# Two PSUM tiles of one bank each for the attention values and the softmax denominators, in place of one tile of two banks

## The chip, the cores and the metric

The kernel runs on one core of a Trainium2 chip. The metric is the time of one execution in microseconds (us) on the device, lower is better. A profile is one further execution, recorded by the hardware profiler. The engines are PE (TensorE, matmuls), PEld (its weight loads), DVE (VectorE), ACT (ScalarE), POOL (GpSimd) and SP (SyncE, which issues all DMAs here).

## What is computed

Attention over a band of neighbours and block summaries, then a GELU feed-forward layer on the result (the inputs q and k are scaled up by 8):

```python
k_sum = k.reshape(B, H, nb, 32, D).max(axis=3); v_sum = v.reshape(B, H, nb, 32, D).mean(axis=3)
scores_l = where(|i - j| < 16, q @ k.T / sqrt(D), -1e9)
scores_s = q @ k_sum.T / sqrt(D) + log(32)
a = softmax(concatenate([scores_l, scores_s], axis=-1))
x = a @ concatenate([v, v_sum], axis=2)          # B, H, S, D = 4, 8, 768, 64
h = x.reshape(B * S, 512) @ w_in                 # 512 x 2048
return gelu(h) @ w_out                           # 2048 x 512
```

## The kernel before

**Tiling.** The 3072 rows are cut into 12 chunks of 256 rows. Attention is done in 24 units: one unit is 4 heads of one chunk, so two units make a chunk's 512 columns of x. All products are made of 16-bit parts: an operand a is held as hi(a) + lo(a), and a product is three matmuls (hi hi, hi lo, lo hi).

**Steps of one unit**, by the names of the ORDER string. `scores u` (L653, 48 matmuls) fills the two-bank PSUM tile ps_s. ACT (`evac`, L659) or DVE (`add_mask`, L662) copies it out to s32, POOL takes the maximum over the partitions (`maximum`, L670, one buffer m32), DVE subtracts it (`shift`, L675), ACT takes the exponential (`exponent`, L678) and rounds it to 16 bits (`s_p_hi`, L684), DVE makes the rest (`p_lo`, L687). Then PE makes two things of p:

- `values u` (L717, 48 matmuls) writes the weighted sum of v into the columns 0 to 511 of the PSUM tile ps_v: its first bank.
- `den u` (L725, 4 matmuls with a matrix of ones) writes the denominators, spread over 64 partitions each, into the columns 512 to 1023 of ps_v: its second bank. 14 of the 24 units do this (0 to 7, 9 to 13 and 16). The other ten sum the denominators on POOL (`pden`, L731) and copy them with L736.

The denominators leave through ACT: `norm_den u` (L741) adds eps and copies the second bank to x32, an SBUF tile. DVE transposes it (`norm_take`, L744), takes reciprocals (`norm_rec`, L747), spreads them back (`norm_spread`, L751), and multiplies the first bank of ps_v by them (`norm_mult`, L757), which gives x. x is split by `x_hi` (ACT, L760; L782 where the feed-forward works on sums) and `x_lo` (DVE, L766; L788).

**The feed-forward.** `phase1 c i` (L806 to L808, 24 matmuls of 256 columns) or `product` (L833, seven products in place of eight for a pair of chunks) fills one of four single PSUM banks. ACT takes the GELU (`gelu`, L854) or a copy (`keep`, L839), DVE adds (`h_add`, L845), `g_hi` (ACT, L864) and `g_lo` (DVE, L868) split it, `phase2` (L881 to L883) multiplies by w_out, and `store` (ACT, L886) and `put` (SP) write the chunk out. Weights arrive early, as 64-bit numbers, and DVE turns them into 32-bit ones with integer operations (L372, L377, L381) before they are split.

**What sets the order.** The ORDER string fixes it by hand: each engine gets its instructions in the order in which the string names the steps, and each engine executes its own in order. What an instruction waits for is set by a recording layer from the tiles that it reads and writes. PSUM has eight banks: two for ps_s, two for ps_v, and four for the ring named bank.

Some stretches of the string matter for the change. `den 6 ... scores 7 ... phase1 2 6, values 6, ... norm_den 6, g_hi 2 1, evac 7, ... scores 8` is one, where the denominators are made well ahead of the values. Unit 9 has the same shape: `den 9, ... phase1 3 3, values 9, ... norm_den 9, ... gelu 3 3, exponent 10, ... s_p_hi 10`, and later `p_lo 10, norm_mult 9, ... den 10`. Unit 3: `den 3, ... norm_den 3, ... values 3`. Unit 5: `den 5, norm_mult 4, x_hi 4, ... x_lo 4, add_mask 6, ... values 5, ... norm_den 5`.

## Time and profile before

| | us |
|---|---|
| median of 3 runs | 598.34 (596.81 to 598.61) |
| the profiled execution | 595.35 |
| its span, first to last instruction | 593.6 |
| PE busy | 578.2 (97% of the span) |
| DVE busy | 439.7 (74%) |
| ACT busy | 362.6 (61%) |
| POOL busy | 169.7 (29%) |
| mean granted TensorE clock | 0.996 |

The span is what the profile shows; the profiled execution's own time is 1.75 us more. [...] In the lists of waits, "A <- B: t, n, m" says that A's engine sat idle before A until B had ended, t us in n times, the longest m us. In the timeline a row is start, duration, engine, line, operation, and in brackets the idle time before it and what ended it. In the chain of waits a row is start, duration and the work that the end was waiting for.

### The profile page before, as it was taken

Reading aid. Unit: us, or ns where it says so; the run is one execution under the profiler, and the core shown is the slowest. Engines: PE = TensorE matmul, PEld = TensorE weight load, DVE = VectorE, ACT = ScalarE, POOL = GpSimd, SP = SyncE. Lnnn points to the kernel's source line nnn. Section 1 sums busy time; section 2 is a strip of 40 time slices with the busy share of each in tenths; the row PEclk is TensorE's granted clock in tenths of the full one; section 3 lists DMA queues with packets and bytes.
Section 4 is the critical chain, followed back from the end, with each engine's and each line's share of the span. In section 5 each row is a group of like instructions: output and inputs, shape, how many; then the busy total and the mean of one; then the engine's idle time right before and its main releaser. Section 6 shows DMA issues by size and latency. Waiting matters only on the chain.

```text
span 593.6 us, 13319 instructions
## 1 busy us (share of the span) xinstructions
PE 578.2 (97%) x5801; PEld 376.5 (63%) x5801; DVE 439.7 (74%) x544; ACT 362.6 (61%) x534; POOL 169.7 (29%) x80
## 2 busy tenths in 40 slices
PE   8999999999899999999999799999999999999997
PEld 3447787444776774588664478755678654686645
DVE  5998999997799989889868778868758665542220
ACT  3899766263776578368882578983675752345410
POOL 3231002023034423115064436453642552100000
PEclk9999999999999999999999999999999999999999
DMA  8765655556557613320231342202112100000001
GB/s 331 277 245 178 212 175 196 180 166 231 164 157 208 205 38 92 114 68 14 65 102 42 106 129 84 81 6 88 43 49 62 37 8 35 19 19 1 1 18 54
DMA packets 27306, 63.78 MB, mean 107 GB/s; under 512 B 2480, under 2 KB 6704, under 8 KB 26672
## 3 DMA queue, kind: packets, MB, share of 16 engines
q1 hardware_dynamic: 27248, 62.93, 33.2%
q8 instruction: 45, 0.74, 0.5%
q14 instruction: 13, 0.11, 0.1%
HBM read 54.86 MB, written 6.29 MB: 103 GB/s over the span
## 4 chain that ended last, share of the span: by engine, by line
PE 79%; ACT 7%; DVE 5%; DMA 3%; POOL 2%; issue 2%; SPq 1%; ACTq 0%; POOLq 0%; DVEq 0%
PE bank L833 22%; PE bank L881 11%; PE bank L883 10%; PE bank L882 10%; PE bank L806 5%; PE bank L807 5%; PE bank L808 5%; PE ps_v L717 3%; PE ps_s L653 3%; DMA v<-in_vw_dram 1%; PE ps_v L725 1%; POOL m L670 1%; DVE v_lo L693 1%; DMA w_out_l<-in_kp_first_dram 1%; POOL m L731 1%
## 5 line engine op out<-in xcount | busy, mean ns | idle before, releaser
L881 PE MATMUL bank<-w_out_h,gh 128*128 128x512 f16 x368 | 139.6, 379 | 0.0
L883 PE MATMUL bank<-w_out_h,gl 128*128 128x512 f16 x368 | 139.5, 379 | 0.0
L882 PE MATMUL bank<-w_out_l,gh 128*128 128x512 f16 x368 | 139.5, 379 | 0.0
L670 POOL PARTITION_ALL_REDUCE m<-s x24 | 82.0, 3417 | 188.4 <-ACT s L659 92.1
L868 DVE SCALAR_TENSOR_TENSOR gl<-g,gh 128x512 f16<-128x512 f32 x96 | 67.1, 712 | 40.3 <-ACT gh L864 40.3
L731 POOL PARTITION_ALL_REDUCE m<-s x10 | 62.0, 6199 | 64.6 <-ACT s L678 64.6
L833 PEld LDWEIGHTS <-w 128*128 128x128 f16 x640 | 62.0, 98 | 11.1 <-issue 1.3
L883 PEld LDWEIGHTS <-gl 128*128 128x128 f16 x368 | 36.0, 98 | 43.8 <-DVE gl L868 0.4
L833 PEld LDWEIGHTS <-w_in 128*128 128x128 f16 x576 | 55.6, 98 | 10.4 <-issue 1.8
L881 PEld LDWEIGHTS <-gh 128*128 128x128 f16 x368 | 36.0, 98 | 39.8 <-issue 1.2
L845 DVE TENSOR_TENSOR g<-bank,late 128x512 f32<-128x512 f32 x48 | 32.8, 686 | 37.5 <-PE bank L833 20.0
L882 PEld LDWEIGHTS <-gh 128*128 128x128 f16 x368 | 36.0, 98 | 38.3
L864 ACT ACTIVATE gh<-g 128x512 f16<-128x512 f32 x96 | 58.4, 624 | 1.0
L839 ACT ACTIVATE late<-bank 128x512 f32<-128x512 f32 x48 | 28.2, 590 | 45.6 <-PE bank L833 34.3
L807 PE MATMUL bank<-x,w_in 128*128 128x256 f16 x192 | 53.0, 276 | 0.8 <-DVE x L766 0.8
L806 PE MATMUL bank<-x,w_in 128*128 128x256 f16 x192 | 53.1, 276 | 0.6 <-ACT w_in L435 0.4
L808 PE MATMUL bank<-x,w_in 128*128 128x256 f16 x192 | 52.9, 276 | 0.0
L833 PE MATMUL bank<-x,w_in 128*128 128x256 f16 x384 | 46.6, 273 | 1.7 <-DVE x L788 1.6
L854 ACT ACTIVATE g<-bank 128x512 f32<-128x512 f32 x48 | 28.1, 592 | 27.8 <-PE bank L808 20.5
L833 PE MATMUL bank<-stage,w 128*128 128x256 f16 x320 | 44.0, 273 | 0.0
L833 PE MATMUL bank<-x,w 128*128 128x256 f16 x320 | 43.9, 273 | 0.0
L854 ACT ACTIVATE g<-g 128x512 f32<-128x512 f32 x48 | 29.7, 624 | 18.4 <-DVE g L845 18.1
(145 smaller groups left out, 1135.9 us busy)
## 6 DMA issues: line engine op xcount, KB each, us to landing
v<-in_vw_dram SPq DMA_DIRECT2D x24, 512.0 KB, 3.6
stage<-in_w_out_dram SPq DMA_DIRECT2D x8, 1024.0 KB
q<-in_qd_dram SPq DMA_DIRECT2D x24, 256.0 KB, 2.8
out_dram<-ot SPq DMA_DIRECT2D x23, 256.0 KB, 2.1
k<-in_kd_dram SPq DMA_DIRECT2D x18, 320.0 KB, 4.9
stage<-in_kp_dram SPq DMA_DIRECT2D x6, 768.0 KB, 4.7
stage<-in_vb_dram SPq DMA_DIRECT2D x6, 768.0 KB
stage<-in_w_in_dram SPq DMA_DIRECT2D x4, 1024.0 KB
```

The source lines that it names most:

```text
L670: nc.gpsimd.partition_all_reduce(out_ap=m32, in_ap=self.s32, channels=P, reduce_op=bass_isa.ReduceOp.max)
L731: nc.gpsimd.partition_all_reduce(out_ap=m32, in_ap=self.s32, channels=P, reduce_op=bass_isa.ReduceOp.add)
L806: nc.tensor.matmul(dst, wh, xh, start=(k == 0), stop=False)
L807: nc.tensor.matmul(dst, wh, xl, start=False, stop=False)
L808: nc.tensor.matmul(dst, wl, xh, start=False, stop=(k == NCC - 1))
L833: nc.tensor.matmul(dst, l, r[:, k], start=(first and e == 0 and k == 0 and n == 0), stop=(k == KH - 1 and n == 2), skip_group_check=True,)
L854: nc.scalar.activation(g, h, AF.Gelu, scale=1.0 / (SC_X * SC_WI))
L864: nc.scalar.activation(gh, g_ring.use(f"{c}_{i}", g_uses(c, i)), AF.Copy, scale=SC_G)
L868: nc.vector.scalar_tensor_tensor(out=gl, in0=g_ring.use(f"{c}_{i}", g_uses(c, i)), scalar=SC_G, in1=gh, op0=ALU.mult, op1=ALU.subtract)
L881: nc.tensor.matmul(t, gh[:, f, js], w_out_h[:, f, :], start=(n == 0), stop=False)
L882: nc.tensor.matmul(t, gh[:, f, js], w_out_l[:, f, :], start=False, stop=False)
L883: nc.tensor.matmul(t, gl[:, f, js], w_out_h[:, f, :], start=False, stop=(n == NFC - 1))
```

## The change

The PSUM tile ps_v of 1024 columns becomes two tiles of 512 columns, ps_v for the values and ps_d for the denominators. Each is one bank; the eight banks are used as before.

```diff
     ps_s = ps.tile([P, UCOLS], F32, name="ps_s")
-    ps_v = ps.tile([P, UCOLS], F32, name="ps_v")
+    ps_v, ps_d = (ps.tile([P, QCOLS], F32, name=n) for n in ("ps_v", "ps_d"))
...
                 for e in range(2):
                     nc.tensor.matmul(
-                        ps_v[e * D : (e + 1) * D, QCOLS:], ones, p[:, e * QCOLS : (e + 1) * QCOLS],
+                        ps_d[e * D : (e + 1) * D], ones, p[:, e * QCOLS : (e + 1) * QCOLS],
                         start=(n == 0), stop=(n == 1),
                     )
...
         def norm_den(self):
-            nc.scalar.activation(self.x32, ps_v[:, QCOLS:], AF.Identity, bias=eps)
+            nc.scalar.activation(self.x32, ps_d, AF.Identity, bias=eps)
...
-            nc.vector.tensor_tensor(out=self.x32, in0=ps_v[:, :QCOLS], in1=dent, op=ALU.mult)
+            nc.vector.tensor_tensor(out=self.x32, in0=ps_v, in1=dent, op=ALU.mult)
```

No instruction is added or removed, and the order on every engine stays. What 40 instructions wait for differs between the two programs. In the rows below a wait names the engine whose count is waited for, not the instruction; which instruction it is, is said in words. Numbers behind a name are buffer numbers and differ by one because there is a tile more.

On ACT, from the GELU ahead of `norm_den 6` (L741) to the one behind `evac 7` (L659), before:

```order
L854 ACTIVATE g_3_100<-bank_65 128x512 [waits PE_49]
L854 ACTIVATE g_0_97<-bank_66 128x512
L741 ACTIVATE den_81<-ps_v,eps 128x512 [waits PE_49]
L864 ACTIVATE gh_101<-g_0_97 128x512 [waits Activation_49]
L659 ACTIVATE s_1_91<-ps_s,logb 128x1024
L854 ACTIVATE g_2_99<-bank_64 128x512
```

and after:

```order
L854 ACTIVATE g_3_101<-bank_66 128x512 [waits PE_49]
L854 ACTIVATE g_0_98<-bank_67 128x512
L741 ACTIVATE den_82<-ps_d,eps 128x512 [waits PE_49]
L864 ACTIVATE gh_102<-g_0_98 128x512 [waits Activation_49]
L659 ACTIVATE s_1_92<-ps_s,logb 128x1024 [waits PE_49]
L854 ACTIVATE g_2_100<-bank_65 128x512 [waits PE_49]
```

Before, `norm_den 6` waits for the last matmul of `values 6`; after, for the last matmul of `den 6`. The two rows behind it had no wait of their own, since the later count covered them; now each waits for its own matmuls (`scores 7` and `phase1 2 6`). The same replacement is made for `norm_den` 5, 9, 10 and 13.

On PE, `den 10` (L725) behind a `phase2` step, before:

```order
L882 MATMUL bank_65<-w_out_l,gh_103 128x512
L883 LDWEIGHTS gl_104
L883 MATMUL bank_65<-w_out_h,gl_104 128x512
L725 LDWEIGHTS ones [waits DVE_49]
L725 MATMUL ps_v<-p_h,ones 64x512 [waits Activation_49]
L725 LDWEIGHTS ones
L725 MATMUL ps_v<-p_h,ones 64x512
L725 LDWEIGHTS ones
L725 MATMUL ps_v<-p_l,ones 64x512
```

and after:

```order
L882 MATMUL bank_66<-w_out_l,gh_104 128x512
L883 LDWEIGHTS gl_105
L883 MATMUL bank_66<-w_out_h,gl_105 128x512
L725 LDWEIGHTS ones
L725 MATMUL ps_d<-p_h,ones 64x512 [waits Activation_49]
L725 LDWEIGHTS ones
L725 MATMUL ps_d<-p_h,ones 64x512
L725 LDWEIGHTS ones
L725 MATMUL ps_d<-p_l,ones 64x512 [waits DVE_49]
```

The wait at the first weight load was for `norm_mult 9` (L757), which reads the values of the unit before. It is gone; what is left of DVE is the wait for `p_lo 10`, at the matmul that reads it. The wait for `norm_mult` of the unit before stands at the first matmul of `values 10` now. `den` 3, 9 and 11 change in the same way. `values 3` waited for `norm_den 3` and now waits for `norm_mult 2`; `values 1` likewise.

On DVE, `norm_mult 4` (L757) to `add_mask 6` (L662), before:

```order
L751 STREAM_TRANSPOSE dent<-rec 128x512 [waits DVE_49]
L757 TENSOR_TENSOR den_81<-ps_v,dent 128x512 [waits DVE_49,PE_49]
L449 TENSOR_TENSOR w_2_77<-w_2_77 128x512
L766 TENSOR_TENSOR x<-den_81,x 128x512 [waits Activation_49]
L662 SCALAR_TENSOR_TENSOR s_0_90<-mask_sb,ps_s 128x1024
```

and after:

```order
L751 STREAM_TRANSPOSE dent<-rec 128x512 [waits DVE_49]
L757 TENSOR_TENSOR den_82<-ps_v,dent 128x512 [waits DVE_49,PE_49]
L449 TENSOR_TENSOR w_2_78<-w_2_78 128x512
L766 TENSOR_TENSOR x<-den_82,x 128x512 [waits Activation_49]
L662 SCALAR_TENSOR_TENSOR s_0_91<-mask_sb,ps_s 128x1024 [waits PE_49]
```

Before, `norm_mult 4` waits for the last matmul of `den 5`, the next unit's; after, for that of `values 4`. `add_mask 6` gets a wait for `scores 6` of its own. `norm_mult` 0 and 7 change likewise.

## The prediction

> **What bounds the kernel now.** I read the page first, then PE's list of waits.

> ```profile
> span 593.6 us, 13319 instructions
> PE 578.2 (97%) x5801; PEld 376.5 (63%) x5801; DVE 439.7 (74%) x544; ACT 362.6 (61%) x534; POOL 169.7 (29%) x80
> ```

> PE is busy for all but 15.4 us of the span, and the other engines are idle for a quarter of it and more. The change takes no work off PE, so it can gain only what PE stands idle and what the idling brings with it. PE's list of waits says where that is:

> ```profile
> PE ps_s L653 <- ACT s L659: 2.3, 1, 2.3
> PE bank L833 <- DVE x L788: 1.6, 1, 1.6
> PE ps_s L653 <- DVE ql L642: 1.3, 1, 1.3
> PE ps_v L725 <- DVE stage L757: 1.3, 1, 1.3
> PE ps_v L717 <- ACT den L741: 1.2, 2, 0.8
> ...
> PE bank L807 <- DVE x L766: 0.8, 1, 0.8
> ```

> Two rows name ps_v itself: `den` waiting for `norm_mult` (1.3) and `values` waiting for `norm_den` (0.8, and the remaining 0.4). These pairs touch different halves of ps_v. The first row, the largest wait of all, and the last, for x, stand at the end of chains that start at L741. What ACT waits for ahead of L741 (the list for that line) shows it:

> ```profile
>   PE ps_v L717: 8.4, 5
>   PE ps_v L725: 0.8, 1
> ```

> L741 reads the denominators, which L725 makes, and yet it stands 8.4 us for L717, the values. So the old tile is waited for as a whole. The question is which of these 8.4 us PE pays for.

> **The change, part by part.** No work is added, so every term is a wait. I go through the places in order of time.

> *At 40 us (`values 1`).* The 0.4 us wait goes, but I count nothing for it. ACT sets this stretch: four microseconds later PE's weight load stands behind ACT's copy of v_lo.

> ```profile
> 45.03 0.41 PEld L430 LDWEIGHTS bank<-w,mask_sb 128*128 128x128 f32 x2 [0.33 <-ACT v_lo L708]
> ```

> A PE that is 0.4 us early waits 0.4 us longer there. Cover gone, this would be a gain of 0.4.

> *At 63 us (`values 3`).* The timelines of PE and ACT:

> ```profile
> 63.79 0.22 PE L717 MATMUL ps_v<-p_h,v_hi 128*64 128x64 f16 x2 [0.79 <-ACT den L741]
> ```
> ```profile
> 61.60 0.63 ACT L760 ACTIVATE x<-den 128x512 f16<-128x512 f32 x1
> ```

> Now `values 3` waits for `norm_mult 2`, whose result ACT's `x_hi 2` (L760) already read at 61.60, so nothing holds it: 0.8 us gained. PE must then find its inputs 0.8 us earlier. DVE, busy with weight bits in the stretch that follows, is the one that could refuse; the meeting that I check is `p_lo 4` (L687) for `den 4`, on DVE's timeline and in the chain:

> ```profile
> 123.19 1.22 DVE L687 TENSOR_TENSOR p_l<-s,p_h 128x1024 f16<-128x1024 f32 x1
> ```
> ```profile
> 125.61 0.55 PE ps_v L725 x4
> ```

> It ends at 124.41, while `den 4` starts on PE at 125.61. 1.2 us of slack against 0.8: the gain passes.

> *At 147 us (`x` of unit 5).* DVE's timeline, then ACT's:

> ```profile
> 136.64 0.70 DVE L751 STREAM_TRANSPOSE dent<-rec 128x512 f32<-128x512 f32 x1
> 139.01 0.69 DVE L757 TENSOR_TENSOR den<-ps_v,dent 128x512 f32<-128x512 f32 x1 [1.68 <-PE ps_v L725]
> ```
> ```profile
> 142.59 0.69 ACT L741 ACTIVATE den<-ps_v,eps 128x512 f32<-128x512 f32 x1 [1.11 <-PE ps_v L717]
> ```

> `norm_mult 4` (139.01) waited 1.68 us for `den 5`, which it doesn't read, and `norm_den 5` (142.59) for `values 5`. Both waits go: DVE is 1.68 us early up to `add_mask 6`, and ACT, free from 141.48 (it sat idle for 1.11 us ahead of 142.59), is at least 1.1 us early with the denominators. x then comes 1.1 to 2.8 us (1.68 + 1.11) early. PE stood 0.8 for it (L807), and with the 0.8 from 63 us it asks for it 1.6 us early: 0.8 gained.

> *At 160 us (`scores 8`).* The chain:

> ```profile
> 154.91 0.55 PE ps_v L725 x4
> ...
> 159.91 0.69 ACT den L741
> 160.60 0.52 ACT gh L864
> 161.12 1.01 ACT s L659
> ```
> ```profile
> 155.14 1.07 ACT L854 ACTIVATE g<-bank 128x512 f32<-128x512 f32 x2
> 159.91 0.69 ACT L741 ACTIVATE den<-ps_v,eps 128x512 f32<-128x512 f32 x1 [3.70 <-PE ps_v L717]
> ```

> `norm_den 6` holds ACT for 3.70 us although `den 6` was done at 155.46. Queued behind it on ACT are `g_hi 2 1` and `evac 7`, and `evac 7` is what frees ps_s for `scores 8`. With the new wait ACT goes on at 156.21, and 0.69 + 0.52 + 1.01 later, at 158.4, ps_s is free. PE gets to `scores 8` when `values 6` ends, just ahead of 159.91. So all 2.3 us go, with 1.5 us to spare. If PE comes 1.6 us early and ACT not at all, 0.1 of it is lost; I take 0.3 off the sum for meetings of this kind.

> The same wait has a second price, which the windows show:

> ```profile
> 159.27:162.68 3.41, 1.11 (x73) 1.08 (x69) 1.53 (x3) 2.77 (x5) 0.47 (x1) 1.00 0.41 76
> 162.68:166.09 3.41, 3.41 (x39) 2.45 (x32) 3.31 (x5) 0.97 (x2) 3.41 (x3) 0.50 0.93 254
> ...
> 333.34:336.76 3.42, 1.79 (x15) 1.29 (x14) 3.42 (x5) 0.30 (x2) 0.03 (x1) 1.00 0.00 0
> ```

> The column behind the busy times of the five engines is the granted clock. It is 0.50 for 3.41 us right behind the idle time. 3.41 us at half speed do 1.7 us of work, so 1.7 us are lost. A stretch of equal length at 333 us in which PE idled for half the time (1.79 busy) was followed by no drop; the one at 159 us with two thirds idle was. With the wait gone the drop should go: 1.7 gained.

> [...]

> *At 227 us (`den 10`).* The chain, ACT's timeline, then DVE's:

> ```profile
> 219.92 0.91 PE ps_v L717 x48
> ```
> ```profile
> 217.05 0.61 ACT L864 ACTIVATE gh<-g 128x512 f16<-128x512 f32 x1
> 220.85 0.69 ACT L741 ACTIVATE stage<-ps_v,eps 128x512 f32<-128x512 f32 x1 [3.19 <-PE ps_v L717]
> 221.43 0.59 ACT L854 ACTIVATE g<-bank 128x512 f32<-128x512 f32 x1
> ```
> ```profile
> 225.50 1.23 DVE L687 TENSOR_TENSOR p_l<-s,p_h 128x1024 f16<-128x1024 f32 x1 [1.01 <-ACT p_h L684]
> 226.64 0.68 DVE L757 TENSOR_TENSOR stage<-ps_v,dent 128x512 f32<-128x512 f32 x1
> ```

> `den 10` no longer waits for `norm_mult 9` (ends 227.32). It still needs `p_lo 10`, which ended at 226.7; that alone would save 0.6 of the 1.3. But ACT too is released: `norm_den 9` can start at 217.66, and the GELU behind it (221.43) no longer stands behind `values 9` (48 matmuls, 0.91) and L741 (0.69): its own matmuls end ahead of them. It, the exponential and `p_hi 10` come 1.5 us earlier, `p_hi 10` ends near 224.0 (`p_lo 10` at 225.50 waited for it), `p_lo 10` near 225.2. `den 10` stood 1.3 us and had begun to wait at 227.34 - 1.3 = 226.0, so PE finds it done: 1.3 gained. Next late is nothing on ps_v: `values 10` needs `norm_mult 9`, near 225.9 then, and is reached 2 us later.

> *Elsewhere* (`norm_den` 10 and 13, `den` 9 and 11, `norm_mult` 0 and 7) PE stood for none of them, and 0 is taken. The two waits of 1.6 and 1.3 in PE's list (L788, L642) belong to a chain at 297 to 341 us; it starts from PE's own work, so it moves with PE and stays as long as it is.

> The sum: 0.8 + 0.8 + 2.3 + 1.7 + 1.3 - 0.3 = 6.6 us. Against the profiled execution that is 595.35 - 6.6 = 588.75. The median before is 598.34, 3.0 us over the profiled one, so the forecast is 598.34 - 6.6 = 591.7.

> **The rivals.**

> *The slow clock stays.* The waits go and the 1.7 us do not, because the drop has another cause or because the timed executions before mostly had none: a fixed grid of 3.41 us stretches may cut the 2.3 us gap in two. [...] Against it: one drop, right behind the largest gap. Gain 4.9, time 593.4.

> *The gain is given back at 297 to 341 us.* There PE ends up waiting for a chain through ACT, POOL and DVE. If an earlier transfer or POOL, not PE, sets when that chain starts, PE only waits longer there, and the end stays: 598.3. The same time comes out if the new waits do not act as the program says. Against it, the start of that chain:

> ```profile
> 295.08 1.43 PE bank L833 x12
> 296.52 0.02 issue
> 296.54 0.04 ACT late L839
> ```

> It hangs on PE's matmuls, then on ACT.

> *DVE is blocked more often by POOL: slower.* When waits go, POOL's reductions start at other times relative to DVE's work, and DVE instructions that run into one are stretched:

> ```profile
> L693 DVE SCALAR_TENSOR_TENSOR v_lo<-v,v_hi x21: 1210/1217/5395, 58.0 to 500.2; 128x1024 f16<-128x1024 f32 x21
> ```

> The longest took 5395 ns in place of 1217: 4.2 us. Each such hit that lands on the chain at 297 to 341 us, where PE already waits for DVE, costs 4.2; it decides from 6.6 + 1.8 = 8.4 us, so from the second hit on, and three give 591.7 + 12.6 = 604.3. Against it: behind the last place above, at 227 us, all engines have moved by nearly the same time, and the hits should stay where they are.

> **How the numbers follow.** The forecast has 0.60, the slow clock that stays 0.24, the gain given back 0.11, the blocked DVE 0.05. About 0.3% (1.8 us) is what a measurement of this kernel can tell from no change. The first two are faster by more than that: 0.84; same 0.11; slower 0.05. The low end is 588.7: 591.7 less the 0.3 and 0.4 that I took off or left out, and less 2.3 of the 3.0 us between profile and median, which could shrink when one slow stretch is gone. The high end reaches past 593.4 to 596.0, which takes in the case that only the 160 us wait is won (598.34 - 2.3). This leaves out the third and fourth case, 0.16.

> **What would show it.** In the profile after: L717 gone from what L741 waits for; no wait of PE on L659 near 155 us, and none on L757 or L741; PE idle near 10 us in place of 15.4; a granted clock of 1.00 throughout behind the start; the waits on L788 and L642 still there, 6 to 7 us earlier. I am wrong if these waits go and the later ones grow by as much, or if PE's list of waits still names ps_v.

## The result and the profile after

The changed kernel takes 587.77 us (median of four executions, 586.85 to 588.23), the kernel before beside it 597.58 (four, 595.25 to 598.61). The ratio is 0.9839 with a 95% interval of 0.9805 to 0.9873: 9.8 us less, where I had forecast 6.6 less. It is 0.9 us below the low end of my range. The profiled execution after took 588.23 us, 7.1 less than the one before.

The page's first lines and PE's list of waits, of the kernel after:

```profile
span 586.4 us, 13321 instructions
PE 576.3 (98%) x5801; PEld 375.7 (64%) x5801; DVE 440.0 (75%) x544; ACT 362.3 (62%) x534; POOL 169.6 (29%) x80
```
```profile
PE bank L833 <- DVE x L788: 1.6, 1, 1.6
PE ps_s L653 <- DVE ql L642: 1.3, 1, 1.3
...
PE ps_v L717 <- ACT v_lo L708: 0.5, 1, 0.5
PE bank L704 <- ACT v_hi L690: 0.5, 1, 0.5
```

PE is idle for 10.1 us (586.4 - 576.3) in place of 15.4. The rows on L659, L741, L757 and L766 are gone. The two waits at the end that I had said would stay, on L788 and L642, are as long as they were. Two new waits of 0.5 us each stand near 40 us, of which I had said nothing; they turn out to be the interesting ones. What ACT waits for ahead of L741 is one row now, where L717 stood with 8.4 us:

```profile
  PE ps_d L725: 0.8, 1
```

At 160 us ACT goes straight through `norm_den 6` (L741), `g_hi 2 1` and `evac 7` (L659). ACT's timeline, and then the windows of the same stretch, with the granted clock behind the five busy times:

```profile
154.68 0.69 ACT L741 ACTIVATE den<-ps_d,eps 128x512 f32<-128x512 f32 x1
155.25 0.64 ACT L864 ACTIVATE gh<-g 128x512 f16<-128x512 f32 x1
155.77 1.12 ACT L659 ACTIVATE s<-ps_s,logb 128x1024 f32<-128x1024 f32 x1
```
```profile
156.34:159.75 3.41, 3.41 (x113) 2.96 (x112) 3.41 (x6) 2.18 (x4) 2.77 (x1) 1.00 0.34 70
159.75:163.16 3.41, 3.41 (x29) 2.58 (x27) 3.31 (x5) 0.96 (x2) 1.67 (x3) 1.00 0.91 239
```

PE never stops there, and the clock stays at 1.00 up to the end. The last place that I had named as a danger, the chain at 297 to 341 us, simply moved with PE. The row of `product` that waits for L788 in both timelines, before and then after:

```profile
335.10 1.36 PE L833 MATMUL bank<-x,w_in 128*128 128x256 f16 x11 [1.63 <-DVE x L788]
```
```profile
327.98 1.36 PE L833 MATMUL bank<-x,w_in 128*128 128x256 f16 x11 [1.64 <-DVE x L788]
```

It is 7.1 us earlier and waits as long as it did. So the profile agrees with each step. Where do the other 2.7 us come from, by which the two medians are further apart than the two profiled executions? The main place where the traces differ in a way that the change doesn't make is DVE's first step on a block of weights (L372), before and after:

```profile
33.02 0.69 DVE L372 TENSOR_SCALAR w<-gh 128x1024 int32<-128x1024 int32 x1 [0.45 <-DMA gh<-in_w_in_dram]
```
```profile
35.43 1.75 DVE L372 TENSOR_SCALAR w<-gh 128x1024 int32<-128x1024 int32 x1 [2.86 <-DMA gh<-in_w_in_dram]
```

The same transfer, issued at 27.0 us in both, landed 2.4 us later in the execution after. Nothing in the change touches that transfer, and between 40 and 45 us it set PE's starts in the execution after back by 1.5 us. The experiments show that it is also the key to the rest.

### The profile page after: what moved, and what is told of

Its sections match the earlier page's. It is cut to its first block, busy times and chain, and to the rows that moved or that the text cites. A ratio compares the mean times of both kernels' runs of the same rounds, so it can differ in the third digit from the quotient of the medians.

```text
span 586.4 us, 13321 instructions
## 1 busy us (share of the span) xinstructions
PE 576.3 (98%) x5801; PEld 375.7 (64%) x5801; DVE 440.0 (75%) x544; ACT 362.3 (62%) x534; POOL 169.6 (29%) x80
## 4 chain that ended last, share of the span: by engine, by line
PE 83%; DVE 5%; ACT 4%; DMA 4%; POOL 2%; issue 1%; SPq 1%; POOLq 0%; DVEq 0%; ACTq 0%
PE bank L833 23%; PE bank L881 12%; PE bank L883 11%; PE bank L882 11%; PE bank L806 5%; PE bank L807 5%; PE bank L808 5%; PE ps_v L717 3%; PE ps_s L653 3%; DMA gh<-in_w_in_dram 1%; PE ps_d L725 1%; POOL m L670 1%; DVE v_lo L693 1%; DMA w_out_l<-in_kp_first_dram 1%; POOL m L731 1%
## 5 line engine op out<-in xcount | busy, mean ns | idle before, releaser
L670 POOL PARTITION_ALL_REDUCE m<-s x24 | 82.5, 3436 | 180.3 <-ACT s L659 100.6
L731 POOL PARTITION_ALL_REDUCE m<-s x10 | 62.0, 6199 | 64.6 <-ACT s L678 64.6
L833 PEld LDWEIGHTS <-w 128*128 128x128 f16 x640 | 62.0, 98 | 10.5 <-issue 0.6
L833 PEld LDWEIGHTS <-w_in 128*128 128x128 f16 x576 | 55.6, 98 | 10.4 <-issue 1.8
L864 ACT ACTIVATE gh<-g 128x512 f16<-128x512 f32 x96 | 58.4, 625 | 1.0
L839 ACT ACTIVATE late<-bank 128x512 f32<-128x512 f32 x48 | 28.2, 589 | 46.9 <-PE bank L833 35.6
L806 PE MATMUL bank<-x,w_in 128*128 128x256 f16 x192 | 52.4, 273 | 0.4 <-ACT w_in L435 0.4
L807 PE MATMUL bank<-x,w_in 128*128 128x256 f16 x192 | 52.4, 273 | 0.0
L833 PE MATMUL bank<-x,w_in 128*128 128x256 f16 x384 | 46.6, 273 | 1.8 <-DVE x L788 1.6
L854 ACT ACTIVATE g<-bank 128x512 f32<-128x512 f32 x48 | 28.1, 591 | 29.6 <-PE bank L808 22.3
L833 PE MATMUL bank<-stage,w 128*128 128x256 f16 x320 | 44.0, 273 | 0.0
L833 PE MATMUL bank<-x,w 128*128 128x256 f16 x320 | 43.9, 273 | 0.0
L854 ACT ACTIVATE g<-g 128x512 f32<-128x512 f32 x48 | 29.7, 624 | 18.4 <-DVE g L845 18.1
```

Of the source, the lines that this page charges most:

```text
L670: nc.gpsimd.partition_all_reduce(out_ap=m32, in_ap=self.s32, channels=P, reduce_op=bass_isa.ReduceOp.max)
L731: nc.gpsimd.partition_all_reduce(out_ap=m32, in_ap=self.s32, channels=P, reduce_op=bass_isa.ReduceOp.add)
L806: nc.tensor.matmul(dst, wh, xh, start=(k == 0), stop=False)
L807: nc.tensor.matmul(dst, wh, xl, start=False, stop=False)
L833: nc.tensor.matmul(dst, l, r[:, k], start=(first and e == 0 and k == 0 and n == 0), stop=(k == KH - 1 and n == 2), skip_group_check=True,)
L854: nc.scalar.activation(g, h, AF.Gelu, scale=1.0 / (SC_X * SC_WI))
```

## The experiments

My first theory was the prediction's own: the gain is made by ACT's released wait at 160 us (2.3 us), the slow stretch behind it (1.7), and three smaller places. The rivals were a slow stretch with another cause, and a gain that comes from PE's own waits on the readers of ps_v. Beside the first four kernels, the kernel before took 594.85 us (median of 29 executions, 593.09 to 598.96).

**`evac 7` ahead of `norm_den 6`, with the tile not split.**

```diff
-gelu 2 1, norm_den 6, g_hi 2 1,
-evac 7, load_k 9,
+gelu 2 1, evac 7, norm_den 6, g_hi 2 1,
+load_k 9,
```

> The kernel before with its one tile ps_v; only evac 7 (L659) now stands ahead of norm_den 6 on ACT, so that it no longer stands behind the wait for values 6. My theory (the wait at 160 us costs PE 2.3 us, and the slow clock behind it 1.7): 4.0 us less than before, a ratio near 0.9933, no wait of PE on L659 and a granted clock of 1.00 at 160 to 166 us. Rival A (the slow clock has another cause): 2.3 less, ratio 0.996, and a stretch at 0.50 still in the profile. Rival B (the loss at 160 us is given back later, and the gain of the split comes from other places): within 1 us of before.

Measured: 593.56 us, ratio 0.9996 (0.9968 to 1.0023): no change that can be told, which looks like rival B. The wait on L659 and the slow stretch were gone from the profile, but PE's timeline had a new wait just behind:

```profile
164.87 0.39 PE L883 MATMUL bank<-w_out_h,gl 128*128 128x512 f16 x1 [1.17 <-DVE gl L868]
```

My edit had left `g_hi 2 1` behind the wait for `values 6`, and now that was late. The edit, not the theory, was incomplete; it is made whole further down.

**`norm_den 6` made to wait for `values 6` again, in the changed kernel.**

```diff
         def norm_den(self):
+            if self.u in (6,): nc.scalar.activation(held, ps_v[:, :1], AF.Copy)
             nc.scalar.activation(self.x32, ps_d, AF.Identity, bias=eps)
```

> The changed kernel, with one more ACT instruction, a copy of one column of ps_v, ahead of norm_den 6 alone, so that norm_den 6 waits for values 6 again. My theory: PE waits on L659 again for some 2.3 us, the clock drops to 0.50 for 3.41 us behind it, and the time is 4.0 us above the changed kernel (about 591.8 against 587.8; 5.8 us less than before). Rival A (the drop was no consequence of the gap): 2.3 above, 590.1. Rival B (the gain is not made at 160 us): no more than 1 us above the changed kernel.

Measured: 590.5 us (588.81 to 592.12), ratio to before 0.9923 (0.9894 to 0.9952). PE's waits and the windows of its profile:

```profile
PE ps_s L653 <- ACT s L659: 2.4, 1, 2.4
```
```profile
155.59:159.01 3.42, 1.28 (x52) 1.03 (x51) 0.80 (x2) 2.10 (x4) 0.00 (x0) 1.00 0.57 137
159.01:162.42 3.41, 3.19 (x57) 2.61 (x57) 3.41 (x5) 1.69 (x4) 3.15 (x2) 0.50 0.92 233
```

The wait comes back with its size and the slow stretch with it. The time rises by 3.1 over the 587.41 of the changed kernel in a later run (not measured beside this one), not by 4.0. Two of its six executions lie at 588.81 and 589.53, below the rest, with a granted clock of 1.000; the other four have 0.997, and one stretch of 3.41 us at a granted clock of 0.50 takes 0.003 off the mean (1.7 of 588.5 us). The median alone lies nearer to rival A's 590.1; the stretch in the profile speaks against A. My theory holds for the mechanism, but the 1.7 us are not paid in every execution.

**All five released `norm_den` held again.** The same line with `(5, 6, 9, 10, 13)`.

> The changed kernel with such a copy ahead of norm_den 5, 6, 9, 10 and 13, the five that the split let go ahead of values; den and values stay free of one another's readers. My theory: the terms at 147 us (0.8), 160 us (2.3 and 1.7) and about 0.7 of the 1.3 at 227 us come back, 5.5 us above the changed kernel, 593.3; what stays of the gain is the 0.8 at 63 us, 0.6 at 227 us and whatever lies between the profiled and the timed executions of before. Rival (half and more of the gain is PE no longer waiting for the readers of ps_v): no more than 3 us above the changed kernel.

Measured: 593.37 us (591.07 to 595.1), ratio 0.997 (0.9947 to 0.9992). The theory's 593.3; the rival (3 us at most) falls. Its waits show the places, and 0.4 us for `den 10` at 227 us:

```profile
PE ps_s L653 <- ACT s L659: 2.4, 1, 2.4
...
PE bank L807 <- DVE x L766: 0.8, 1, 0.8
...
PE ps_d L725 <- DVE p_l L687: 0.4, 1, 0.4
```

**Matmuls in the gap at 160 us, in the kernel before.** The change is `fill 6` ahead of `scores 8`, where

```diff
+    fill = lambda n: [nc.tensor.matmul(bank.free[0][0:D], ones, ones.unsqueeze(1).broadcast_to([P, DM // D, D]), start=True, stop=True) for _ in range(n)]
```

> The kernel before, with six more matmuls (ones by ones, 512 columns, into a free bank that nothing reads before it is written again) on PE between values 6 and scores 8: the wait for evac 7 stays, but PE works for about 1.3 of its 2.3 us. My theory (the idle time is what takes the clock down): no stretch at 0.50 behind 160 us, 1.7 us less than before, ratio near 0.997, with scores 8 starting when it did. Rival A (the drop comes from something else, such as the load on the chip at that time): the stretch stays, and so does the time. Rival B (the filler delays scores 8): as before or slower by up to 1 us.

Measured: 593.57 us (592.88 to 597.26), ratio 0.9994 (0.9969 to 1.002). In the profiled execution PE still waited 1.0 us for L659 at 160 us, and no slow stretch followed. That fits the theory, but this one profile can't prove it, as the last section shows: a boundary at 165.52 us, counted in steps of 3.413 us from the slow stretch at 42.64, cut this gap, and by an estimate (2.86 us busy, less the 1.28 that the filler added) PE would have been busy for 1.58 us of the window ahead of it without the filler, between the 1.48 that a slow stretch followed in the runs below and the 1.64 that none followed. The twelve times say more. The time did not fall as a whole: eight executions lie between 592.88 and 593.75, and four at 596.88 to 597.26, with nothing between, where 14 of the 29 of the kernel before lie, most of them near 595 with a granted clock of 0.997. The first edit had shown the same: seven at 592.81 to 593.66, five at 596.76 to 597.49. The profiled execution of the filler run was of the upper four, and its profile tells why. DVE's, ACT's and PE's timelines near 40 us, and the windows:

```profile
35.64 1.70 DVE L372 TENSOR_SCALAR w<-gh 128x1024 int32<-128x1024 int32 x1 [3.20 <-DMA gh<-in_w_in_dram]
```
```profile
39.82 0.63 ACT L760 ACTIVATE x<-den 128x512 f16<-128x512 f32 x1 [2.00 <-DVE den L757]
...
42.04 0.69 ACT L741 ACTIVATE den<-ps_v,eps 128x512 f32<-128x512 f32 x1
```
```profile
42.78 0.26 PE L717 MATMUL ps_v<-p_h,v_hi 128*64 128x64 f16 x2 [2.51 <-ACT den L741]
```
```profile
39.23:42.64 3.41, 1.05 (x3) 0.20 (x2) 3.41 (x5) 2.77 (x5) 0.00 (x0) 1.00 0.51 186
42.64:46.06 3.42, 3.28 (x51) 2.02 (x51) 3.34 (x6) 3.05 (x5) 1.29 (x1) 0.50 0.00 0
```

Read them from the top. The weights landed late, so DVE, which takes its instructions in order, stood for 3.20 us, and `norm_mult 0` behind it was late. ACT's `x_hi 0` waited 2.00 us for that, and `norm_den 1` (L741) stands behind `x_hi 0` on ACT. With one tile, `values 1` on PE must wait until `norm_den 1` has read the old contents: 2.51 us in place of the 0.4 that the profile before showed. PE was busy for only 1.05 of 3.41 us, and a slow stretch followed that costs 1.7 more.

So the place at 40 us, for which I had counted nothing, costs one of two amounts in these two profiles, and the difference is 2.1 + 1.7 = 3.8 us. The second theory is this: before's times fall into groups by the landing of that transfer and by the slow stretch at 160 us, and the split takes both away. The rival is that the groups have nothing to do with the tile.

**The changed kernel again, unaltered.**

> The changed kernel once more, unaltered, beside many executions of before. The times of before fall into groups: about 593.3 us (clock 1.000 throughout), 595.0 (one slow stretch), 596.9 (one slow stretch) and 598.7 (two). The theory that I form from the profile of the filler run: there are two places that differ from one execution to the next. At 40 us a transfer of weights lands at 33.0 or at 35.5 us, and where it lands late, norm_den 1 is late and values 1 of the one tile stands 2.5 us for it, with a slow stretch behind (3.8 us in all); at 160 us the wait is followed by a slow stretch or not (1.7). The split should take both away: then the changed kernel has clock 0.999 to 1.000 and two close groups, early landing near 587, late landing near 588 (PE waits 0.5 and 0.5 for ACT's copies instead), spread under 2 us. Rival (the groups have nothing to do with the tile): the changed kernel has groups over 3 us apart as well.

Measured: 587.41 us, ratio 0.9851 (0.9824 to 0.9878). Its six times are 586.46, 586.62, 586.70 and 588.12, 588.14, 588.19; before beside it ran from 592.99 to 598.77. Two groups 1.5 us apart, where before has a spread of 5.8. The profiled execution, 588.14, has a late landing (L372 at 34.88) and PE's two waits of 0.5.

**The fetch put ahead, in the kernel before and in the changed one.** The transfer that lands early or late is issued at 14.4 us in place of 27.0 in both:

```diff
-wi_diff 1 1, load_q 3, s_q_hi 3,
+wi_diff 1 1, load_q 3, fetch_w_in 2, s_q_hi 3,
...
-wi_diff 0 1, fetch_w_in 2, fetch_w_in 5,
+wi_diff 0 1, fetch_w_in 5,
```

> The kernel before, with the fetch of weights that lands early or late (fetch_w_in 2) put two places further ahead in SP's queue, ahead of load_v 1, which it stands behind until 27 us; nothing is written to its tile earlier, so it can go at about 14.5 us. Theory: always landed when DVE asks for it, so the groups at 596.9 and 598.7 are gone; what is left is 593.3 and 595.0, the latter with the stretch at 160 us. Rival (the late group has another cause, such as the traffic of that time as a whole): a group above 596 stays. A third way: the fetch now collides with transfers that the start waits for, and all times rise by up to 2 us.

> The changed kernel with the same fetch put ahead. Theory: only the early landing is left, so near 587 us with a spread under 1 us, some 0.5 to 1 us less than the changed kernel's median; beside the same edit in before (593.3 or 595.0) the split is then worth 6.4 to 8.1 us. Rival: the fetch costs the start as much as it wins, 588 or more.

Measured: before with this edit 594.97 us, ratio 0.9975 (0.9955 to 0.9995); all twelve executions lie between 592.92 and 595.42, four of them below 593.7. Of nineteen executions of the unedited kernel beside it eight lie above 595.9, of these none. The changed kernel with it takes 586.47 us (586.42 to 587.17), ratio to before 0.9838 (0.9813 to 0.9864), 0.9 less than the changed kernel as it was. DVE's row in the first of the two, which now waits for nothing, and then PE's at `values 1`:

```profile
32.48 0.68 DVE L372 TENSOR_SCALAR w<-gh 128x1024 int32<-128x1024 int32 x1
```
```profile
40.47 0.22 PE L717 MATMUL ps_v<-p_h,v_hi 128*64 128x64 f16 x2 [0.40 <-ACT den L741]
```

The upper groups are gone, as the theory says. Against this early landing, PE's starts in the filler's profile fall back by 2.1 us at `values 1` and by 1.5 in the slow stretch, 3.6 in place of the 3.8 that I had reckoned. The two kernels can now be compared with the same landing: 594.97 - 586.47 = 8.5 us.

**Only `norm_den 6` moved back on ACT, with the tile not split.** The first edit made whole: `gelu 2 1, g_hi 2 1, evac 7, norm_den 6`.

> The kernel before; on ACT both g_hi 2 1 and evac 7 now stand ahead of norm_den 6 (in the first version of this run only evac 7 did, and g_hi 2 1 stayed behind the wait). Theory: PE's wait at 160 us (2.3 us) and the slow stretch behind it are gone, g_hi is in time, so the groups are 591.0 (in place of 593.3 and 595.0) and 594.7 (in place of 596.9 and 598.7). Rival A (what is won at 160 us is given back later): 593.3 and 596.9, as with evac 7 alone, with a new wait of PE of 1 us and more. Rival B (the slow stretch has another cause): four groups, each 2.3 us lower.

Measured: 592.37 us, ratio 0.9942 (0.9915 to 0.9968); the lower executions are 591.41, 591.56 and 591.86, one at 595.68. The wait on L659 and the slow stretch were gone:

```profile
158.24:161.65 3.41, 3.41 (x114) 2.96 (x112) 3.41 (x4) 1.37 (x3) 2.68 (x1) 1.00 0.53 189
```

The lowest are 1.4 to 1.9 us below before's 593.3, not 2.3. Set against the profile of before, PE gains 2.4 us at `scores 8` and 1.6 behind it, and loses 0.9 again by 183 us, 0.5 of it at `values 7`, which stood 0.4 for `p_lo 7` (L687). So the wait and the slow stretch do go with ACT's release alone, and without the split 0.9 us of it is given back. Rival B falls for this place, and rival A for all but these 0.9 us.

**The landing made late in both kernels.** `fetch_w_in 5, fetch_w_in 2` in place of `fetch_w_in 2, fetch_w_in 5`.

> The kernel before with two neighbours in SP's queue swapped (fetch_w_in 5 ahead of fetch_w_in 2), so that the weights that DVE asks for at 32.6 us always land late, 34.5 us or later. Theory: the low groups are gone; values 1 stands 1.3 to 3 us for norm_den 1, mostly with a slow stretch behind, and the times are 596.5 to 599.5, some 3.8 us above the same kernel with the early landing (593.3 and 595.0). Rival (the landing is hidden, and the late groups come from something else): 593.3 and 595.0 stay the commonest times.

> The changed kernel with the same swap, so the same late landing. Theory: values 1 no longer stands for norm_den 1, so PE waits only for ACT's copies (0.5 and 0.5, or up to 1 more if the landing is later than in any run so far), no slow stretch: 588 to 589, 8.5 to 10.5 us less than before with the swap, against 8.5 between the two kernels with the early fetch (6.9 where before had no slow stretch). Rival (the split does nothing for the late landing): 590.5 or more, the same 3.8 us above 586.5 as before shows.

Measured: before 600.38 us (599.3 to 601.56 in twelve executions), ratio 1.0055 (1.0034 to 1.0075); the changed kernel 589.09 us (588.05 to 590.86), ratio 0.9867 (0.9837 to 0.9896). PE's timeline and windows, the one tile:

```profile
43.87 0.26 PE L717 MATMUL ps_v<-p_h,v_hi 128*64 128x64 f16 x2 [3.83 <-ACT den L741]
```
```profile
38.56:41.97 3.41, 1.48 (x18) 0.59 (x10) 3.24 (x6) 1.06 (x2) 0.00 (x0) 1.00 0.47 178
41.97:45.38 3.41, 1.51 (x49) 1.36 (x48) 3.41 (x5) 3.36 (x5) 0.00 (x0) 0.50 0.00 0
45.38:48.80 3.42, 3.42 (x5) 1.33 (x5) 3.25 (x6) 1.98 (x5) 2.94 (x1) 0.50 0.00 0
164.85:168.26 3.41, 1.11 (x73) 1.08 (x69) 1.50 (x3) 2.74 (x5) 0.44 (x1) 1.00 0.16 37
168.26:171.68 3.42, 3.42 (x41) 2.47 (x34) 3.31 (x5) 0.99 (x2) 3.42 (x3) 0.50 0.95 231
```

PE's timeline, two tiles:

```profile
40.95 0.22 PE L717 MATMUL ps_v<-p_h,v_hi 128*64 128x64 f16 x2 [0.89 <-DVE den L757]
42.09 0.22 PE L717 MATMUL ps_v<-p_h,v_lo 128*64 128x64 f16 x2 [0.90 <-ACT v_lo L708]
```

The landing was later than in any other run (L372 at 37.14 and 36.82), so both are somewhat above what I expected. Against the early fetch, the late landing costs 600.38 - 594.97 = 5.4 us with one tile and 589.09 - 586.47 = 2.6 with two. (The early and the late runs were not measured side by side; the traces, by PE's starts, give 5.7 and 3.0 behind 48 us.) The split is worth 8.5 us with the early landing and 11.3 with this late one.

**`values 1` held behind `norm_den 1` again, in the changed kernel.**

```diff
             nc.scalar.activation(self.x32, ps_d, AF.Identity, bias=eps)
+            if self.u in (1,): nc.scalar.activation(held, ps_v[:, :1], AF.Copy)
```

> The changed kernel with a copy of one column of ps_v by ACT right behind norm_den 1, so that values 1 waits for norm_den 1 again; everything else stays split. Theory: about 0.5 above the changed kernel where the transfer lands early (587.0), and 1.4 to 3.2 above where it lands late (589.5 to 591.3, the more where a slow stretch follows). Rival (my prediction's own working: what is won at 40 us is lost at 45 us): the same times as the changed kernel, 586.5 and 588.1.

Measured: 589.24 us (587.29 to 590.5), ratio 0.9864 (0.9834 to 0.9893), 1.8 over the 587.41 of the changed kernel, which was not measured beside it. Two of its six executions lie at 587.29 and 588.01, four at 589.12 to 590.50. My prediction's working for this place, named as the rival, falls. The profiled execution (589.35, landing at 35.00), in PE's timeline and in the windows:

```profile
42.80 0.22 PE L717 MATMUL ps_v<-p_h,v_hi 128*64 128x64 f16 x2 [2.57 <-ACT held L742]
```
```profile
37.72:41.13 3.41, 2.52 (x54) 1.26 (x52) 3.24 (x6) 1.38 (x4) 0.84 (x1) 1.00 0.83 318
41.13:44.54 3.41, 1.74 (x51) 1.23 (x51) 3.41 (x5) 3.38 (x5) 0.00 (x0) 1.00 0.03 9
44.54:47.96 3.42, 3.42 (x12) 1.53 (x10) 3.22 (x6) 3.18 (x7) 3.17 (x1) 1.00 0.21 48
```

A gap of 2.57 us, longer than the one at 160 us, and no slow stretch. The last section comes back to that.

**All of PE's waits put back, ACT's left released.** The line above with `(1, 3)`, and behind `norm_mult`

```diff
+            if self.u in (2, 8, 9, 10): nc.vector.tensor_copy(out=held_v, in_=ps_d[:, :1])
```

> The changed kernel with the waits of den and values put back (values 1 and 3 behind ACT's reading of ps_v, den 3, 9, 10 and 11 behind norm_mult, by copies of one column), and norm_den 5, 6, 9, 10 and 13 left free of values. Theory: what comes back is the 40 us place as with values 1 alone (0.5, or 1.4 to 3.2), 0.8 to 0.9 at 63 us, and little at 227 us, since ACT is early there: 588 with the early landing, 590.4 to 592.2 with the late one. Rival (the waits of ACT carry nearly all): within 0.5 us of the changed kernel.

Measured: 590.13 us (588.58 to 592.16), ratio 0.9885 (0.9853 to 0.9917). The theory had 588, and 590.4 to 592.2; two executions lie at 588.6, three at 590.62 to 592.16, and one between, at 589.63. The rival falls. PE's timeline at `values 1` and `values 3`:

```profile
40.63 0.22 PE L717 MATMUL ps_v<-p_h,v_hi 128*64 128x64 f16 x2 [0.70 <-ACT held L742]
...
64.06 0.22 PE L717 MATMUL ps_v<-p_h,v_hi 128*64 128x64 f16 x2 [0.84 <-ACT held L742]
```

There is no wait of `den 10` at 227 us in its list, though `den 10` stands behind `norm_mult 9` again: ACT's release alone is enough for the whole of that place, as I had expected.

## Why the prediction was right in its places and wrong in its sum

The two kernels with the fetch put ahead have the same landing and the same order of instructions. How far PE was ahead in the second, taken from the starts of the same instructions in the two traces, sets each term beside what it measured:

| place | forecast | measured |
|---|---|---|
| 40 us, `values 1` | 0 | 0.45 |
| 63 us, `values 3` | 0.8 | 0.98 |
| 147 us, x of unit 5 | 0.8 | 1.32 |
| 160 us, `scores 8` | 2.3 | 2.37 |
| slow stretch behind it | 1.7 | 1.60 |
| 227 us, `den 10` | 1.3 | 1.37 |
| meetings with late engines | -0.3 | 0 |
| elsewhere (0.19 ahead of 40 us, 0.23 at 336 us) | 0 | 0.42 |
| sum | 6.6 | 8.5 |

The two terms of the last row but one are not in the pair of profiles before and after, so they may be differences of the two executions and not of the kernels.

*Right.* Each place that I named gained, the three largest terms within 0.1 us, and nothing was given back: PE's lead never falls by more than 0.04 us along the whole program. The rival at 297 to 341 us found no trace, nor did the one on POOL in that place (the v_lo step on L693 took 5.40 us there before and 5.39 after); at 40 us a DVE step that took 1.75 us in place of 0.69 beside POOL does play a part, as told below. That the slow stretch follows from idle PE time is shown by the run with `norm_den 6` held (it is back), and the times of the filler run agree (the executions near 595 are gone while the wait stays). The rival that it would stay is answered: it went, together with the wait. Its doubt, that the timed executions might not all have the stretch, was justified: with the early landing 8 of 12 executions of before lie at 594.65 to 595.42 with a granted clock of 0.997, and 4 at 592.92 to 593.64 with 0.999 or 1.000, 1.7 us lower.

*Wrong, first:* the step at 40 us. I argued that PE, 0.4 us early, would wait 0.4 us longer for ACT's copy at 45 us. It kept the 0.45 with the early landing. The row that I rested it on was the weight load behind ACT's copy of v_lo, 0.33 us idle. With the tile split and the early landing the same load comes 0.63 us earlier than with one tile and is idle for the same 0.33 us (PE's weight loads, then ACT's copy):

```profile
44.45 0.41 PEld L430 LDWEIGHTS bank<-w,mask_sb 128*128 128x128 f32 x2 [0.33 <-ACT w_in L387]
```
```profile
44.06 0.61 ACT L708 ACTIVATE v_lo<-bank 128x512 f16<-128x512 f32 x1
```

The copy of v_lo ends at 44.67 there, behind the start of the load, so the load doesn't wait for it, and ACT did not hold PE. At 147 us I counted the wait on L807 and left out the smaller one on L806 in the same place. In the run with ACT held they stand at 0.77 and 0.30.

*Wrong, above all:* the step "The median before is 598.34, 3.0 us over the profiled one, so the forecast is 598.34 - 6.6". Of the 3.9 us between 591.7 and the measured 587.8, the places make 1.9 (8.5 against 6.6), and this step the other 2.0. I took the distance between the profiled and the timed executions for something that both kernels have (the low end of the range let 2.3 of the 3.0 us go, for one slow stretch, which was not enough). It was a second price of the same shared tile, which the profiled execution happened not to pay. There the weights had landed at 33.0 us and `values 1` stood 0.4 us; with a landing at 35.6 us it stands 2.5 us, and a slow stretch may follow. The runs with the early and with the late landing show that this is what separates before's groups, and that the split takes most of it away: the late landing costs the changed kernel 1.5 us (588.1 against 586.6, in the two waits of 0.5 and what they push back) and, in its profiles, no slow stretch.

The granted clock of the timed executions agrees: with the landing made late it is 0.991 or 0.994 in all twelve of before, two or three slow stretches (the profiled one, at 0.991, shows three), and 0.997 or more in all six of the changed kernel. Not every execution of the changed kernel is free of a slow stretch: three of the sixteen with the usual or the early landing show 0.997 (587.40, 588.19 and 587.17 us), at a cost under 1 us against the others of their group, and so does the slowest of the late six (590.86); none of the four was profiled, so where it lies is open. The three timed executions before (596.81, 598.34, 598.61) lie where the late landing puts them; as they have no traces of their own, that it was so in each of them is inferred, not seen. With mostly late executions before and mixed ones after, 9.8 us lie between the 8.5 and 11.3 of the two pairs.

Why a small difference in the landing makes such groups shows in a step that I had overlooked. POOL's `maximum` (L670) starts at 34.4 to 34.9 us in every profile. Where DVE's L372 starts ahead of it, L372 takes 0.68 to 0.70 us (seven profiles); where it starts behind, 1.29 to 2.30 (the other seven). The two that lie closest are the run with `norm_den 6` moved back and the changed kernel measured again:

```profile
34.64 0.69 DVE L372 TENSOR_SCALAR w<-gh 128x1024 int32<-128x1024 int32 x1 [2.13 <-DMA gh<-in_w_in_dram]
34.72 3.70 POOL L670 PARTITION_ALL_REDUCE m<-s  x1 [13.10 <-ACT s L659]
```
```profile
34.72 3.70 POOL L670 PARTITION_ALL_REDUCE m<-s  x1 [13.11 <-ACT s L659]
34.88 2.28 DVE L372 TENSOR_SCALAR w<-gh 128x1024 int32<-128x1024 int32 x1 [2.37 <-DMA gh<-in_w_in_dram]
```

A landing 0.24 us later ends the step 1.8 us later. So 0.6 to 1.6 us of the lateness that reaches `values 1` is this stretching, the one of my POOL rival in another place: in the profile before, L693's step of 5.40 us (median 1.22) started at 314.73 us, behind POOL's L731 at 314.32. No run moves POOL's step, so that POOL causes it is not shown by an experiment; the fourteen profiles agree with it without exception.

What decides when that transfer lands is open. It was issued at 27.0 us in the early and in the late execution alike, beside other transfers, and I have not looked for more than the way to keep it out: the changed kernel with the fetch put ahead, 586.47 us, is the fastest version here.

## What to carry to other kernels

A wait that costs 0.4 us in one profile can cost ten times as much when a transfer ahead of it lands late (0.40 and 3.83 here), so for a shared tile ask how much later its reader could come, not only how late it came. When timed executions lie above the profiled one, or fall into groups, look for the place that makes the groups before taking the distance for an offset; a place that the change touches is the first to suspect. An experiment that moves one instruction must carry along what stands behind it in the same queue, or it measures its own new wait (1.17 us in the first edit).

## What the runs showed of the hardware

```profile
322.90:326.31 3.41, 1.64 (x15) 1.09 (x13) 2.46 (x4) 1.73 (x4) 1.63 (x2) 1.00 0.06 22
326.31:329.72 3.41, 3.41 (x22) 2.10 (x22) 3.38 (x5) 0.53 (x1) 0.00 (x0) 1.00 0.04 5
```

Of the windows at full clock in these rows, the busiest that a slow stretch followed had 1.48 us of PE work, and the least busy that none followed 1.64: 43% and 48% of a window. The length of the gap alone doesn't order them: one of 2.30 us inside one window (159.87 to 162.17 in before, in 159.27 to 162.68) was followed by 0.50, and one of 2.57 us (40.23 to 42.80 where `values 1` was held, with a counted boundary at 41.13) by 1.00. This would also explain why the same kernel pays 1.7 us in one execution and not in the next: where the windows lie against the program differs. By an estimate from these rows (a slow stretch where PE is idle for at least 1.8 to 1.9 us of one window), a gap of 2.30 us would be followed by one at 54 to 63% of the positions; with the early landing 8 of 12 executions of before have the lower clock. No execution without the stretch at 160 us, and without the filler, was traced with the gap in place, so this stays inferred.

*A price of the split that I had not listed:* none was seen. `values` and `den` now write two tiles, and no list of waits of the changed kernel, in any run, names a reader of the other one.
